# Softmax backward by row sums of P∘dP on VectorE instead of a product with O^T on TensorE, in a transformer block's backward pass

## The chip, the cores and the metric

The kernel runs on one core of one Trainium2 chip. The metric is device time in microseconds (us) of one execution, from launch to end. The engines are TensorE (PE, with its weight loads shown as PEld), VectorE (DVE), ScalarE (ACT), GpSimd (POOL) and SyncE (SP); SP and POOL also issue DMA transfers, in the order of their own queues, and a queue that waits for something holds everything behind it. One matmul reads its stationary operand (lhsT) as a weight load and streams the other (rhs) through the array.

## The reference, cut to what matters

One adaLN-modulated block, forward and all gradients: x + ga·A(h1), then x + gb·GLU(h2). A is attention over 64 segments of 32 tokens with a memory of 8 rows that the previous segment's output feeds, so segments follow each other, forward and, in reverse, backward.

```
for s in range(n_seg):                       # 64 segments, 32 heads of 128, L = 8 + 32 rows
    h = concat([mem, x[s]]);  q, k, v = h@Wq, h@Wk, h@Wv
    p = softmax(q k^T * scale + mask);  o = p v
    o = einsum(o, Wo);  mem = o[:8];  outs += o[8:]
# backward of one head's softmax, with dO given:
dV = P^T dO;  dP = dO V^T
dS = P * (dP - rowsum(P * dP)) * scale       # rowsum(P*dP) equals rowsum(O * dO)
dQ = dS K;  dK = dS^T Q;  dh = dQ Wq^T + dK Wk^T + dV Wv^T
```

The weight gradients (wgrad) of Wo, Wq, Wk, Wv are products over all 64·40 rows, made in a last phase.

## The kernel before, in words

The 32 heads are packed three to a group of 120 rows: 11 groups (`G`), each a 128x128 tile of a 128x1408 array. `PG = 4` groups share one PSUM bank, so work per segment goes in three parts (`NP = 3`) of 4, 4 and 3 groups.

**Phases.** Phase 2 is the forward pass, 64 segments in a row. For each it stores to DRAM the V^T columns (`VT`), the probabilities (`PS`), rows of Q and K (`QST`, `KST`), rows of O (`OSR`) and O^T (`OT`). Phase 3 is the GLU, forward and backward, a software pipeline of seven stages over 16 tiles of 128 rows, and its weight gradients. Phase 4 is attention backward, segments 63 down to 0. Phase 5 makes the weight gradients of the four attention matrices and the first layer norm's backward.

**Phase 4, one segment.** `col_pass` projects the incoming gradient dy by Wo^T to rows (`RAd`), `turn_half` transposes them, `to_heads` (ACT and DVE) writes the columns dO^T (`dOT`). POOL copies the rows into `dOst`. Then dP = dO V^T is started in PSUM (`dp`, L1405); DVE multiplies O^T by dO^T in place (`prod`, L1390); and 11 matmuls of that product against a tile of minus ones (`negones`, L1413) subtract rowsum(O∘dO) from dP in the same PSUM bank, so one DVE instruction per part (L1415) gives dS. PE goes on with dV (`grad_part("dVT")`, L1426), the transposes of dS (`dstt`, L1342, copied by DVE, L1440), dK, the product of dV^T with Wv^T (`dht`, L211, 32 column-tiled matmuls), dQ, and `dht` for dK and dQ. `fold_split` and `fold_sum` add the four column tiles and give the memory gradient, which the next segment's dy needs (`dyT`, L1525). dK leaves PSUM by DVE, dV and dQ by ACT.

Every fourth segment completes a batch of memory-row tails: `get_db` (POOL, L1182) copies its input `dyb`, `proj_b` projects it on PE in two halves, in the segments with s % 4 = 2 and 1, and `turn_b` transposes it where s % 4 = 0.

**Row stores.** Each of dV^T, dK^T, dQ^T is turned to rows by a DMA transpose on SP's queue into one of three buffers (`rows_x`), and POOL issues the store to DRAM (`DVR`, `DKR`, `DQR`, L1436). A segment ends with `store_rows_x(2)`, which issues its dV store; the next one issues the dK store after its `dOst` copies (`store_rows_x(1)`) and the dQ store later (`store_rows_x(0)`).

**Order.** In phases 2 and 4 `pin` fixes each engine's order as written. In phase 3 a planner orders the instructions by its own estimates of cost, within their dependencies. There, `s0` computes on POOL `db = dout * gb` (L904) and the reciprocal deviation `rstd` (L917), on which DVE's normalisation (L920) waits.

**Phase 5.** The gradients are made in chunks of at most four heads by 20 row pairs. The first Wo chunk has two heads (`rows_a`, loaded in segment 0 of phase 4 by `p5_first` into the memory of `WoT`), the second the other two of that group; their matmuls are L1744, those of the other three matrices L1731. `ln_tile` loads its own inputs (x0, dh, dx1) where it uses them, and its two small matmuls stand in PE's order between chunks (L1617, L1620).

Of the kernel before, what the change touches and what calls it, by code (L numbers as in the profile page):

```python
# [8 lines left out]
F32 = mybir.dt.float32  # L9
# [31 lines left out]
class K:  # L41
# [43 lines left out]
    def alloc_dram(self):  # L85
# [9 lines left out]
        self.OT = d("OT", GL, BF16)  # L95
# [308 lines left out]
    def phase2(self):  # L404
# [13 lines left out]
        with ExitStack() as ctx:  # L418
# [210 lines left out]
            for s in range(NS):  # L629
# [149 lines left out]
                nc.sync.dma_start(self.OT[s], gl3(OT))  # L779
# [52 lines left out]
    def phase3(self):  # L832
# [9 lines left out]
        with ExitStack() as ctx:  # L842
# [53 lines left out]
            def s0(j):  # L896
# [6 lines left out]
                db = sbp.tile([128, D], BF16, name="db", bufs=2)  # L903
                nc.gpsimd.tensor_tensor(db[:], st["dout"][:], gb_bc[:], op=ALU.mult)  # L904
                nc.gpsimd.dma_start(self.DBROWS[r0:r1, :], db[:])
# [10 lines left out]
                rstd = sbp.tile([128, 1], F32, name="rstd2", bufs=6)  # L916
                nc.gpsimd.tensor_tensor(rstd[:], ve[:], mhalf[:], op=ALU.pow)  # L917
                xh2 = sbp.tile([128, D], BF16, name="xh2", bufs=5)
# [236 lines left out]
    def p4_weights_setup_begin(self):  # L1155
        nc, tc, cfg, io = self.nc, self.tc, self.cfg, self.io
        D, DC, H, E = cfg.D, cfg.DC, cfg.H, cfg.E
        ctx = self.p4_ctx
        self.wo_ctx = ExitStack()
        wop = self.wo_ctx.enter_context(tc.tile_pool(name="p4wo", bufs=1, side="right", reuse_waits="tile"))  # L1160
        self.WoT = wop.tile([128, DC, H * E], BF16, name="WoT")
        wp = ctx.enter_context(tc.tile_pool(name="p4w", bufs=1, side="right", reuse_waits="tile"))
        self.negones = wp.tile([128, 128], BF16, name="negones")
        nc.gpsimd.memset(self.negones[:], -1.0)
        self.WqT = wp.tile([128, H, D], BF16, name="WqT")
        self.WkT = wp.tile([128, H, D], BF16, name="WkT")
        self.WvT = wp.tile([128, H, D], BF16, name="WvT")
        self.dyp = ctx.enter_context(tc.tile_pool(name="p4dy", bufs=3, side="right", reuse_waits="tile"))
        self.dap = ctx.enter_context(tc.tile_pool(name="p4da", bufs=2, side="right", reuse_waits="tile"))
        self.das, self.dbs = {}, {}  # L1170
# [62 lines left out]
    def phase4(self):  # L1233
# [7 lines left out]
        with self.p4_ctx as ctx:  # L1241
            WqT, WkT, WvT, WoT, negones = self.WqT, self.WkT, self.WvT, self.WoT, self.negones

            ldp = ctx.enter_context(tc.tile_pool(name="p4ld", bufs=2, reuse_waits="tile"))
# [28 lines left out]
            btd = pt.tile([128, 8, 128], BF16, name="btd")  # L1273
# [51 lines left out]
            def get_loads(s):  # L1325
                if s not in loads:
                    d = {}
                    for nm, dram in (("OT", self.OT), ("Pst", self.PS)):
                        t = ldp.tile([128, G * GW], BF16, name=nm + "_l")
                        nc.sync.dma_start(gl3(t), dram[s])  # L1330
                        d[nm] = t
# [42 lines left out]
            for s in reversed(range(NS)):  # L1374
# [9 lines left out]
                VT, OT, Pst, Kst, Qst = ld["VT"], ld["OT"], ld["Pst"], Kst_t, Qst_t  # L1384
# [3 lines left out]
                def prod(pi):  # L1388
                    n = min(PG, G - pi * PG)
                    nc.vector.tensor_tensor(part3(OT, pi)[:, :, 0:120],  # L1390
                                            dOT[:, pi * PG * 120:(pi * PG + n) * 120].rearrange("p (g x) -> p g x", x=120),
                                            part3(OT, pi)[:, :, 0:120], op=ALU.mult)
# [7 lines left out]
                def dp(pi):  # L1400
                    ps = dps[pi] = ps_f32("dp_ps")
                    n = min(PG, G - pi * PG)
                    for j in range(n):
                        g = pi * PG + j
                        nc.tensor.matmul(ps[:, j, :], lhsT=dOT[:, g * 120:g * 120 + GW], rhs=VT[:, g * 120:g * 120 + GW],  # L1405
                                         start=(j == 0), stop=False, skip_group_check=True)

                def ds(pi):
                    ps = dps[pi]
                    n = min(PG, G - pi * PG)  # L1410
                    for j in range(n):
                        g = pi * PG + j
                        nc.tensor.matmul(ps[:, j, :], lhsT=OT[:, g * GW:(g + 1) * GW], rhs=negones[:, :],  # L1413
                                         start=False, stop=True, skip_group_check=True)
                    nc.vector.scalar_tensor_tensor(out=part3(dS, pi), in0=ps[:, 0:n, :], scalar=cfg.scale, in1=part3(Pst, pi),  # L1415
                                                   op0=ALU.mult, op1=ALU.mult)
# [13 lines left out]
                def grad_out(nm, xt, pi, eng, ps):  # L1430
                    self.evac(eng, part3(xt, pi), ps[:, 0:min(PG, G - pi * PG), :])
# [30 lines left out]
                if s == 0:  # L1462
                    self.p5_first()
                late = None
# [12 lines left out]
                prod(0)  # L1477
                dp(0)
                prod(1)
                dp(1)  # L1480
                prod(2)
                ds(0)
                self.pop_later()
                dp(2)
                dost(2)
                ds(1)
                ds(2)
# [7 lines left out]
                grad_part("dVT", dOst, Pst, dVT, 0, "act")  # L1495
                grad_part("dVT", dOst, Pst, dVT, 1, "act")
                dstt(0)
                gk0 = grad_mm("dKT", Qst, dS, 0)
                grad_part("dVT", dOst, Pst, dVT, 2, "act")
                dstt(1)  # L1500
                gk1 = grad_mm("dKT", Qst, dS, 1)
                dstt(2)
                gk2 = grad_mm("dKT", Qst, dS, 2)
                load_rows(Qst_t, self.QST, s - 1)
                for pi, g in enumerate((gk0, gk1, gk2)):
                    grad_out("dKT", dKT, pi, "dve", g)
                for pi in range(NP):
                    dht(dVT, WvT, pi)
# [7 lines left out]
                if s > 0:  # L1516
                    store_rows_x(2)
# [25 lines left out]
    def p5_first(self):  # L1543
# [4 lines left out]
        self.rows_a = self.flat(self.WoT, NTP * D, NTP * 2 * E).rearrange("p (t x) -> p t x", t=NTP)  # L1548
# [3 lines left out]
        osr = lambda r, n, tl: self.OSR[:, r:r + n, 0:2, :].rearrange("s (tp tl) g e -> tl s tp (g e)", tl=2)[tl]  # L1552
        for a in (M // 2, M // 2 + tps):
            for tl in range(2):
                n = min(tps, T // 2 - a)
                nc.sync.dma_start(self.rows_a[tl * NS:(tl + 1) * NS, a:a + n, :], osr(2 * a, 2 * n, tl))
                if n < tps:
                    nc.sync.dma_start(self.rows_a[tl * NS:(tl + 1) * NS, a + n:NTP, :], osr(96, 8, tl))
                nc.sync.dma_start(self.dyrows[tl * NS:(tl + 1) * NS, a:a + tps, :],
                                  self.DAROWS[:, :].rearrange("(s tp tl) d -> tl s tp d", tp=T // 2, tl=2)[tl][:, a - M // 2:a - M // 2 + tps])  # L1560
        for tl in range(2):
            nc.sync.dma_start(self.rows_a[tl * NS:(tl + 1) * NS, 0:M // 2, :], osr(0, M, tl))
# [10 lines left out]
    def phase5(self):  # L1573
# [8 lines left out]
        with ExitStack() as ctx:  # L1582
            ctx.enter_context(self.wo_ctx)
            rp = ctx.enter_context(tc.tile_pool(name="p5g_r", bufs=1, side="right", reuse_waits="tile"))
# [16 lines left out]
            def ln_tile(j):  # L1601
                r0, r1 = j * 128, (j + 1) * 128
                x0 = sb2.tile([128, D], BF16, name="x0_5")
                nc.sync.dma_start(x0[:], x_rows[r0:r1, :])
                st = sb1.tile([128, 6], F32, name="st5")
# [9 lines left out]
                dhb = sb2.tile([128, D], BF16, name="dhb5")  # L1615
                self.load_x_rows(dhb, j, self.DHA, self.DHB)
# [4 lines left out]
                dx1 = sb2.tile([128, D], F32, name="dx1_5")  # L1621
                nc.sync.dma_start(dx1[:], self.DX1ROWS[r0:r1, :])
# [49 lines left out]
            if not getattr(cfg, "skip_wgrad", False):  # L1672
# [20 lines left out]
                o_chunks = [(0, 0, 2), (0, 2, 2)] + chunks[1:]  # L1693
# [21 lines left out]
                for i, (_, kind, outw, (hl, g0, ng)) in enumerate(todo):  # L1715
# [6 lines left out]
                    while ln_done[0] * (n_ln - 3) < (i - 3) * NT and ln_done[0] < NT:  # L1722
# [14 lines left out]
                    else:  # L1737
# [3 lines left out]
                        for part in parts:  # L1741
                            for gg in range(ng):
                                for tp_ in part:
                                    nc.tensor.matmul(pss[gg][:], lhsT=rows[:, tp_, gg * E:(gg + 1) * E], rhs=dyrows[:, tp_, :],  # L1744
# [183 lines left out]
```

## Time and profile before

| | |
|---|---|
| median of 7 runs | 3353.46 us (3346.57 to 3359.04) |
| the profiled execution | 3355.38 us; span of its trace 3353.6 us |
| phase 2 | about 39 to 1062 us |
| phase 3, pipeline and its weight gradients | about 1062 to 1645 us |
| phase 4 | about 1645 to 2737 us |
| phase 5 | about 2737 to the end |
| PE busy | 3030.6 us, 90% of the span |
| DVE, ACT, POOL busy | 1629.9, 1136.3, 1432.0 us |
| DMA | 699.38 MB moved, 209 GB/s over the span |
| O^T stores and loads | 64 of each, 352.0 KB each |

A group of the profile names its line, engine, operation, the tiles written and read, the count, the busy time and the mean of one; behind it the engine's idle time before it and what ended that. Overlapping instructions of one engine both count as long as they last, so the distance between two starts is what an instruction costs in a stream, and its duration is what a waiting engine sees.

### The profile page before, as it was taken

Reading aid. Unit: us, or ns where it says so; the run is one execution under the profiler, and the core shown is the slowest. Engines: PE = TensorE matmul, PEld = TensorE weight load, DVE = VectorE, ACT = ScalarE, POOL = GpSimd, SP = SyncE. Lnnn points to the kernel's source line nnn. Section 1 sums busy time; section 2 is a strip of 40 time slices with the busy share of each in tenths; the row PEclk is TensorE's granted clock in tenths of the full one; section 3 lists DMA queues with packets and bytes.
Section 4 is the critical chain, followed back from the end, with each engine's and each line's share of the span. In section 5 each row is a group of like instructions: output and inputs, shape, how many; then the busy total and the mean of one; then the engine's idle time right before and its main releaser. Section 6 shows DMA issues by size and latency. Waiting matters only on the chain. (4 is left out here: it accounts for less than half of the span.)

```text
span 3353.6 us, 95627 instructions
## 1 busy us (share of the span) xinstructions
PE 3030.6 (90%) x38574; PEld 1728.2 (52%) x38650; DVE 1629.9 (49%) x4298; ACT 1136.3 (34%) x2586; POOL 1432.0 (43%) x3037
## 2 busy tenths in 40 slices
PE   6999999999997899989989989998999978999999
PEld 3555555555554444445555555555555543444454
DVE  5556556666554777632345544455455531332211
ACT  3555555555543333322233333333333320110011
POOL 3556555655554555511344434344444431232321
PEclk8999999999998999999999999999999998999999
DMA  8655655555556798887699999999999999789886
GB/s 300 175 165 167 174 170 163 169 170 165 169 165 206 180 212 206 205 261 235 181 243 235 242 239 232 235 233 243 244 238 240 238 223 226 223 183 201 197 223 167
DMA packets 862015, 699.38 MB, mean 209 GB/s; under 512 B 560690, under 2 KB 734274, under 8 KB 861444
## 3 DMA queue, kind: packets, MB, share of 16 engines
q1 hardware_dynamic: 737220, 483.44, 61.3%
q0 software_dynamic: 52912, 147.43, 13.7%
q10 hardware_dynamic: 71440, 62.40, 7.2%
q8 instruction: 304, 4.98, 0.7%
q14 instruction: 139, 1.14, 0.1%
HBM read 293.60 MB, written 275.02 MB: 170 GB/s over the span
## 5 line engine op out<-in xcount | busy, mean ns | idle before, releaser
L1731 PE MATMUL gps<-rows,hrows 128*128 128x512 bf16 (+2 forms) x2124 | 416.9, 356 | 5.5 <-ACT ot L61 2.7
L1731 PEld LDWEIGHTS <-hrows 128*128 128x128 bf16 x2160 | 211.6, 98 | 209.5 <-issue 5.1
L222 PEld LDWEIGHTS <-hT 128*32 128x32 bf16 x6144 | 160.2, 98 | 187.1 <-ACT hT L785 30.5
L1436 POOL DMA_DIRECT2D DVR<-rows_x x64 | 35.7, 558 | 422.6 <-DMA rows_x<-dVT 422.6
L282 DVE TENSOR_TENSOR dh_lo<-dh_ps,dh_hi 128x256 bf16<-128x256 f32 x128 | 48.3, 419 | 317.5 <-ACT dh_hi L278 317.5
L1735 POOL DMA_DIRECT2D out_dram<-ot x108 | 81.2, 753 | 254.4 <-DVE ot L63 144.5
L63 DVE CAST ot<-gps 128x512 bf16<-128x512 f32 (+3 forms) x76 | 47.7, 632 | 261.9 <-PE gps L1731 106.1
L791 POOL TENSOR_TENSOR Pst<-Pst,rden 120x1408 bf16<-120x1408 bf16 x63 | 159.4, 2530 | 16.4 <-issue 8.3
L1744 PE MATMUL gps5o<-WoT,rows 128*128 128x512 bf16 x588 | 135.6, 390 | 22.5 <-DMA rows<-OSR 21.6
L222 PE MATMUL pass_ps<-Wv,hT 128*32 128x512 bf16 x2048 | 126.9, 391 | 24.0 <-ACT hT L785 24.0
L61 ACT ACTIVATE dQT<-g_ps 128x512 bf16<-128x512 f32 (+1 forms) x192 | 94.0, 562 | 157.7 <-issue 136.8
L61 ACT ACTIVATE ot<-gps 128x512 bf16<-128x512 f32 (+3 forms) x75 | 41.1, 548 | 312.2 <-PE gps L1731 131.7
L222 PE MATMUL pass_ps<-WoT,dyT 128*32 128x512 bf16 x2048 | 123.9, 384 | 22.5 <-ACT dyT L1525 22.5
L306 POOL DMA_DIRECT2D AOA<-at_rb x64 | 36.7, 574 | 249.5 <-DVE at_rb L305 135.9
L694 DVE TENSOR_TENSOR Ost<-or_ps,rden 120x512 bf16<-120x512 f32 (+1 forms) x192 | 124.2, 647 | 23.0 <-PE or_ps L692 2.2
L211 PE MATMUL dh_ps<-WvT,dVT 128*32 128x512 bf16 x2048 | 122.9, 382 | 0.0
L211 PE MATMUL dh_ps<-WkT,dKT 128*32 128x512 bf16 x2048 | 122.3, 381 | 0.0
L211 PE MATMUL at_ps<-Wo,OT 128*32 128x512 bf16 x2048 | 122.3, 381 | 0.0
L222 PE MATMUL pass_ps<-Wk,hT 128*32 128x512 bf16 x2048 | 122.2, 381 | 0.0
L211 PE MATMUL dh_ps<-WqT,dQT 128*32 128x512 bf16 x2048 | 121.6, 379 | 0.0
L222 PE MATMUL pass_ps<-Wq,hT 128*32 128x512 bf16 x2048 | 121.6, 379 | 0.0
L1460 POOL COPY dOst<-RAd 96x512 bf16<-96x512 bf16 x128 | 77.4, 616 | 96.5 <-DVE RAd L63 96.5
(409 smaller groups left out, 7295.1 us busy)
## 6 DMA issues: line engine op xcount, KB each, us to landing
OSR<-Ost SPq DMA_DIRECT2D x64, 352.0 KB
OT<-OT SPq DMA_DIRECT2D x64, 352.0 KB
PS<-Pst SPq DMA_DIRECT2D x64, 352.0 KB
OT_l<-OT SPq DMA_DIRECT2D x64, 352.0 KB
Pst_l<-PS SPq DMA_DIRECT2D x64, 352.0 KB
DVR<-rows_x POOLq DMA_DIRECT2D x64, 352.0 KB, 4.8
DKR<-rows_x POOLq DMA_DIRECT2D x64, 352.0 KB, 5.6
DQR<-rows_x POOLq DMA_DIRECT2D x64, 352.0 KB, 5.8
```

The source lines that it names most:

```text
L61: return nc.scalar.activation(out, in_, AF.Copy)
L63: return nc.vector.tensor_copy(out, in_)
L211: self.nc.tensor.matmul(ps[32 * j:32 * j + 32, :], lhsT=lhsT, rhs=w, start=(n < 4), stop=(n >= total - 4), tile_position=(0, 32 * j))
L222: self.nc.tensor.matmul(ps[32 * j:32 * j + 32, :], lhsT=lhs(c), rhs=rhs, start=(c == 0), stop=(c == DC - 1), tile_position=(0, 32 * j))
L282: nc.vector.tensor_tensor(lo[:], ps[:, 256 * h:256 * h + 256], parts[h][:], op=ALU.subtract)
L306: nc.gpsimd.dma_start(dram, rb[:])
L694: nc.vector.tensor_tensor(part3(Ost, pi)[0:120, 0:n, :], or_ps[0:120, 0:n, :], rden[:, pi * PG:pi * PG + n].unsqueeze(2).to_broadcast([120 ...
L791: nc.gpsimd.tensor_tensor(Pst[0:120, :, :], Pst[0:120, :, :], rden[:, :].unsqueeze(2).to_broadcast([120, G, 128]), op=ALU.mult)
L1460: nc.gpsimd.tensor_copy(dOst[0:96, 512 * hf:512 * hf + 512], RAd[0:96, 512 * hf:512 * hf + 512])
L1731: nc.tensor.matmul(ps[:, 0:ng * E], lhsT=hrows[:, tp_, c * 128:(c + 1) * 128], rhs=rows[:, tp_, 0:ng * E], start=(tp_ == 0), stop=(tp_ == ...
L1735: nc.gpsimd.dma_start(outw[c * 128:(c + 1) * 128, h0:h0 + 3 * (ng - 1) + 1:3, :], ot[:, 0:ng * E].rearrange("p (h e) -> p h e", e=E))
L1744: nc.tensor.matmul(pss[gg][:], lhsT=rows[:, tp_, gg * E:(gg + 1) * E], rhs=dyrows[:, tp_, :], start=(tp_ == order[0]), stop=(tp_ == order[ ...
```

## The change

Five parts.

1. O^T is no longer stored in phase 2 nor loaded in phase 4. `prod`, the matmuls with `negones` and the one DVE instruction per part are gone. DVE now makes, group by group, P∘dP with its row sum as an accumulated output (128x128 from PSUM), and then (dP − sum)∘P with that sum as a scalar per row: 22 instructions of 128x128 a segment. The factor `scale` moves to the evacuations of dK and dQ.
2. The order behind it: all three `dp` parts first, then all of `ds`; the dV matmuls; for each part the transposes of dS and dK, with the 32 `dht` matmuls of dV between the second and the third; dK leaves PSUM by ACT instead of DVE.
3. `store_rows_x(2)` at a segment's end is gone: the dV store is issued in the next segment, with the dK store, behind the `dOst` copies.
4. In phase 3 POOL's `db` and its store stand behind `rstd`, and the two instructions are tied in this order.
5. In phase 5 the first Wo chunk has four heads. Of its 20 row pairs 12 are loaded in segment 0 into `WoT`'s memory, two into `btd`, which now lives on into phase 5, and six already in segment 6 (`p5_early`). The layer norm's inputs are loaded one tile ahead (`ln_load`), and its tiles start a chunk later.

```
@@ phase 2
-                nc.sync.dma_start(self.OT[s], gl3(OT))
@@ phase 3, s0
-                db = sbp.tile([128, D], BF16, name="db", bufs=2)
-                nc.gpsimd.tensor_tensor(db[:], st["dout"][:], gb_bc[:], op=ALU.mult)
-                nc.gpsimd.dma_start(self.DBROWS[r0:r1, :], db[:])
...
+                i0 = len(self.traced())
                 nc.gpsimd.tensor_tensor(rstd[:], ve[:], mhalf[:], op=ALU.pow)
+                db = sbp.tile([128, D], BF16, name="db", bufs=2)
+                nc.gpsimd.tensor_tensor(db[:], st["dout"][:], gb_bc[:], op=ALU.mult)
+                self.pin(i0, [mybir.EngineType.Pool])
+                nc.gpsimd.dma_start(self.DBROWS[r0:r1, :], db[:])
@@ phase 4, loads and ds
-                    for nm, dram in (("OT", self.OT), ("Pst", self.PS)):
-                        t = ldp.tile([128, G * GW], BF16, name=nm + "_l")
-                        nc.sync.dma_start(gl3(t), dram[s])
-                        d[nm] = t
+                    d["Pst"] = ldp.tile([128, G * GW], BF16, name="Pst_l")
+                    nc.sync.dma_start(gl3(d["Pst"]), self.PS[s])
...
-                def prod(pi):
-                    n = min(PG, G - pi * PG)
-                    nc.vector.tensor_tensor(part3(OT, pi)[:, :, 0:120],
-                                            dOT[:, pi * PG * 120:(pi * PG + n) * 120].rearrange("p (g x) -> p g x", x=120),
-                                            part3(OT, pi)[:, :, 0:120], op=ALU.mult)
+                rsum = sb2.tile([128, G], F32, name="rsum")
...
                     for j in range(n):
                         g = pi * PG + j
-                        nc.tensor.matmul(ps[:, j, :], lhsT=OT[:, g * GW:(g + 1) * GW], rhs=negones[:, :],
-                                         start=False, stop=True, skip_group_check=True)
-                    nc.vector.scalar_tensor_tensor(out=part3(dS, pi), in0=ps[:, 0:n, :], scalar=cfg.scale, in1=part3(Pst, pi),
-                                                   op0=ALU.mult, op1=ALU.mult)
+                        junk = sb2.tile([128, GW], BF16, name="pdp")
+                        nc.vector.scalar_tensor_tensor(out=junk[:], in0=ps[:, j, :], scalar=1.0, in1=part3(Pst, pi)[:, j, :],
+                                                       op0=ALU.mult, op1=ALU.mult, accum_out=rsum[:, g:g + 1])
+                    for j in range(n):
+                        g = pi * PG + j
+                        nc.vector.scalar_tensor_tensor(out=part3(dS, pi)[:, j, :], in0=ps[:, j, :], scalar=rsum[:, g:g + 1],
+                                                       in1=part3(Pst, pi)[:, j, :], op0=ALU.subtract, op1=ALU.mult)
...
-                    self.evac(eng, part3(xt, pi), ps[:, 0:min(PG, G - pi * PG), :])
+                    nc.scalar.activation(part3(xt, pi), ps[:, 0:min(PG, G - pi * PG), :], AF.Copy,
+                                         scale=1.0 if nm == "dVT" else cfg.scale)
@@ phase 4, order of a segment
+                if s == 6:
+                    self.p5_early()
...
-                prod(0)
                 dp(0)
-                prod(1)
                 dp(1)
-                prod(2)
-                ds(0)
+                dp(2)
+                for pi in range(NP):
+                    ds(pi)
+                dost(2)
                 self.pop_later()
-                dp(2)
-                dost(2)
-                ds(1)
-                ds(2)
...
-                grad_part("dVT", dOst, Pst, dVT, 0, "act")
-                grad_part("dVT", dOst, Pst, dVT, 1, "act")
-                dstt(0)
-                gk0 = grad_mm("dKT", Qst, dS, 0)
-                grad_part("dVT", dOst, Pst, dVT, 2, "act")
-                dstt(1)
-                gk1 = grad_mm("dKT", Qst, dS, 1)
-                dstt(2)
-                gk2 = grad_mm("dKT", Qst, dS, 2)
+                for pi in range(NP):
+                    grad_part("dVT", dOst, Pst, dVT, pi, "act")
+                for pi in range(NP):
+                    dstt(pi)
+                    grad_part("dKT", Qst, dS, dKT, pi, "act")
+                    if pi == 1:
+                        for pj in range(NP):
+                            dht(dVT, WvT, pj)
                 load_rows(Qst_t, self.QST, s - 1)
-                for pi, g in enumerate((gk0, gk1, gk2)):
-                    grad_out("dKT", dKT, pi, "dve", g)
-                for pi in range(NP):
-                    dht(dVT, WvT, pi)
...
-                if s > 0:
-                    store_rows_x(2)
@@ phase 5
-        self.rows_a = self.flat(self.WoT, NTP * D, NTP * 2 * E).rearrange("p (t x) -> p t x", t=NTP)
+        n = NTP - 8
+        self.rows_a = self.flat(self.WoT, NTP * D, n * 4 * E).rearrange("p (t x) -> p t x", t=n)
...
+    def osr_rows(self, r, n, tl):
+        return self.OSR[:, r:r + n, 0:4, :].rearrange("s (tp tl) g e -> tl s tp (g e)", tl=2)[tl]
+
+    def p5_early(self):
+        NS, h = self.cfg.NS, self.cfg.T // 2
+        for tl in range(2):
+            self.nc.sync.dma_start(self.rows_x0[tl * NS:(tl + 1) * NS, 0:4, :], self.osr_rows(2 * (h - 4), 8, tl))
+            self.nc.sync.dma_start(self.rows_x0[tl * NS:(tl + 1) * NS, 4:6, :], self.osr_rows(96, 4, tl))
...
+            def ln_load(j):
+                if j >= NT or j in ln_in:
+                    return
...
             def ln_tile(j):
                 r0, r1 = j * 128, (j + 1) * 128
-                x0 = sb2.tile([128, D], BF16, name="x0_5")
-                nc.sync.dma_start(x0[:], x_rows[r0:r1, :])
+                ln_load(j)
+                ln_load(j + 1)
+                x0, dhb, dx1 = ln_in.pop(j)
...
-                o_chunks = [(0, 0, 2), (0, 2, 2)] + chunks[1:]
+                o_chunks = chunks
...
-                    while ln_done[0] * (n_ln - 3) < (i - 3) * NT and ln_done[0] < NT:
+                    if i == 3:
+                        ln_load(0)
+                    while ln_done[0] * (n_ln - 4) < (i - 4) * NT and ln_done[0] < NT:
                         ln_step()
```

## The prediction

> **What bounds the kernel now.** First the busy time by stage (columns: stretch, its length, then PE, PEld, DVE, ACT and POOL busy with instruction counts, granted TensorE clock, DMA share, GB/s). The rows are phase 2, phase 3's pipeline, phase 4, the turn into phase 5 and the rest.
>
> ```profile
> 39.00:1062.00 1023.00, 945.27 (x16574) 588.52 (x16571) 602.02 (x1896) 517.10 (x1302) 586.09 (x1412) 0.99 0.59 170
> 1062.00:1450.00 388.00, 339.74 (x1897) 167.97 (x1916) 260.08 (x449) 130.73 (x228) 199.94 (x216) 0.96 0.85 213
> 1645.00:2724.00 1079.00, 971.00 (x15680) 576.88 (x15681) 546.83 (x1482) 377.52 (x881) 448.06 (x1109) 0.98 1.06 237
> 2724.00:2923.00 199.00, 163.40 (x939) 74.74 (x949) 48.35 (x114) 18.45 (x33) 43.30 (x66) 0.91 0.93 217
> ```
>
> PE is the busy engine everywhere, so each stage is read by what PE waits for. DMA looks full in phase 4; the waits of PE there (total, times, longest) show that this hardly matters:
>
> ```profile
> PE dp_ps L1405 <- ACT dOT L61: 27.7, 63, 0.5
> PE pass_ps L222 <- POOL dyb L1182: 27.7, 13, 3.4
> PE pass_ps L222 <- ACT dyT L1525: 22.5, 63, 0.9
> PE dp_ps L1413 <- DVE OT_l L1390: 11.1, 56, 0.6
> PE g_ps L1426 <- POOL dOst L1460: 2.7, 4, 1.7
> PE dp_ps L1405 <- DMA VT_l<-VT: 2.5, 1, 2.5
> ```
>
> One wait for DMA in 1079 us. Two of the rows are POOL's lateness. The timeline of one segment shows the stretch that the change rewrites (start, length, engine, line), and below it POOL in another segment:
>
> ```profile
> 1957.74 0.46 PE L1405 MATMUL dp_ps<-VT_l,dOT 128*128 128x128 bf16 x5 [0.46 <-ACT dOT L61]
> 1957.92 0.97 DVE L1390 TENSOR_TENSOR OT_l<-dOT,OT_l 128x480 bf16<-128x480 bf16 x3
> 1958.81 1.75 DVE L1415 SCALAR_TENSOR_TENSOR dS<-dp_ps,Pst_l 128x512 bf16<-128x512 f32 x3
> 1961.59 1.91 PE L211 MATMUL dh_ps<-WvT,dVT 128*32 128x512 bf16 x32
> 1964.15 1.91 PE L211 MATMUL dh_ps<-WkT,dKT 128*32 128x512 bf16 x32
> ...
> 2005.05 0.56 POOL L1436 DMA_DIRECT2D DVR<-rows_x  x1 [9.59 <-DMA rows_x<-dVT]
> 2006.64 0.29 POOL L1182 COPY dyb<-daq 128x128 bf16<-128x128 bf16 x1
> 2006.98 1.05 PE L222 MATMUL pass_ps<-WoT,dyb 128*32 128x512 bf16 x16 [2.67 <-POOL dyb L1182]
> ```
>
> DVE needs 2.7 us for prod and dS, and PE fills them. From the resumed dp (1957.74) to dht of dK (1964.15) PE takes 6.41 us; two other segments show 6.47 and 6.26. The distance from one L1525 to the next gives segment lengths: at best 16.32, 16.43, 16.32 and 15.66 us for s % 4 = 0, 1, 2, 3, but the kind 2 averages 18.85 over 16. All surplus over the best of each kind is 50.5 us, 40.4 of it in kind 2, where POOL stood before the dV store.
>
> **Phase 4: the new row sums.** The price of one small DVE instruction comes from these rows:
>
> ```profile
> 1443.90 0.69 DVE L1015 SCALAR_TENSOR_TENSOR dxh<-mm,Wv 128x512 f32<-128x512 f32 x1 [0.58 <-ACT dh2b L1012]
> 1444.52 0.08 DVE L1015 DVE_READ_ACCUMULATOR dxh<-mm,Wv 128x1 f32 x1
> 1444.52 0.69 DVE L1018 TENSOR_TENSOR pr_cb<-mm,xh 128x512 bf16<-128x512 f32 x1
> 1445.12 0.68 DVE L1021 SCALAR_TENSOR_TENSOR junk<-dxh,xh 128x512 f32<-128x512 f32 x1
> 1445.97 0.74 DVE L1028 SCALAR_TENSOR_TENSOR ta<-dxh,rstd,Wv 128x512 f32<-128x512 f32 x1
> ```
>
> A plain pass of 512 from PSUM lasts 0.69 but the next starts after 0.60, 0.09 sooner; a 128x128 cast from PSUM (L299) lasts 0.289, so 0.20 in a stream. The accumulator adds 0.02 (0.62 against 0.60), a pointer scalar 0.05 (0.74 against 0.69). So the two kinds cost 0.22 and 0.25, mean 0.235; 22 make 5.17 us where prod and dS took 2.7. Bounds: 0.20 if both additions hide, 0.355 if nothing overlaps (0.289 plus 0.08, and 0.289 plus 0.05). I take 0.235, nearest to rows that read PSUM with an accumulator in a stream; each waits only for an instruction two or more back.
>
> Let T be the resumed dp. Its bank is readable at T+0.27 (0.23 of matmul, 0.04 to DVE). Sixteen instructions, two parts of dS, last 3.76, the last result 0.09 more: T+4.12. PE has by then done the rest of dp, dost, dV and the first dstt and dK, and idles some 1.6 us. Then the end of dstt(1) and dK(1) 0.34, dht of dV 1.84 (1961.59 to 1963.43 before), dstt(2) and dK(2) six at 0.057, dQ eleven at 0.057: dht of dK at T+7.27. The 11 negones matmuls (0.63) are already out of this. Against 6.26 to 6.47: +0.9 a segment, **+58 us** over 64; by the bounds +22 and +181. dS(2) and the copies of dS^T (0.34 apart) end about T+7.0, just ahead of the last dQ. In kind 1, DVE's evacuation of RBd stands ahead of the copies and adds 0.1.
>
> dK by ACT (0.6 and 0.55 an instruction): ACT has idle time there (dQT waited 136.8 us on "issue"), and only the last part precedes the dht that needs it; nothing. Its cover gone, 0.55 a segment. SP's dK transpose comes a little over 1 us later, and the Q load now stands behind it; that load has most of a segment until its use: nothing.
>
> **Phase 4: the late store.** What waits behind the dV store on POOL now (tail copies, dyb, dyT, dOst) goes ahead of it. In the segment shown the rows landed 3.35 us after the segment's start; POOL now comes to the store about 4.2 us after it, so the wait mostly ends. Behind it now are the dK store, the DHA store, the copies of the next dO^T tails, the dQ store and the three dOst transfers, needed some 10 us on. The next dV transpose may wait for its buffer by about 1 us, seen by SP alone. Gain between 27.7 (PE's own wait for dyb) and 50.5; I take 45, as dOst and what follows were late in the same segments: **-45 us**.
>
> O^T's stores and loads, 45 MB: PE's waits in phase 2 are compute waits but for 0.4 us, in phase 4 but for 2.5: 0, at most -3.
>
> **Phase 3.** In the pipeline's first tile PE lost 13.4 us:
>
> ```profile
> 1083.28 1.16 POOL L904 TENSOR_TENSOR db<-Wv 128x512 bf16<-128x512 bf16 x1 [7.97 <-DMA Wv<-in_grad_out_dram]
> 1094.31 0.58 POOL L917 TENSOR_TENSOR rstd<-ve,mhalf 128x1 f32<-128x1 f32 x1
> 1094.93 0.55 DVE L920 TENSOR_SCALAR xhf<-x,mv,rstd 128x512 f32<-128x512 f32 x1 [13.89 <-POOL rstd L917]
> ```
>
> Three db stood before the first rstd; now it can run at 1081. What is late next is h's transpose: SP has some 25 loads ahead of it at 0.35 each and now db's transpose too, so about 1094 instead of 1097.9: -4 (0 to -13.4). In the steady loop PE waits for du 22.6 us in 14 times, 0.74 at least: 12.2 to win. junk (L1021) takes 1.20 on average, 0.68 undisturbed: it meets POOL's umh, which now comes some 2 us sooner. -8, between -12 and +8, as db now meets h2a (a DVE pass beside db took 1.65 instead of 0.68). Together **-12**.
>
> **Phase 5.** PE waited 21.6 us for the second chunk's rows, and its next 11 matmuls took 4.85 us instead of 2.4 at the lower clock. Now 80 matmuls (17.3 us) come before a load is needed, but that load is twice as large: the chunk that started at 2786.0 gains only the 0.79 MB loaded early, 3.6 us at 217 GB/s: -4 (+3 to -10). The waits for dhb (8.4) and pr (2.4) go with loading ahead: -10 (0 to -10.8). Together **-14**.
>
> **Sum.** 58 - 45 - 12 - 14 = -13. The profiled execution's own time is 3355.4, so 3342; the median shown is 1.9 lower: 3340.
>
> A rule that speaks against it: the Trainium skill (VectorE: DVE Perf Modes, section "The TRN2 errata — SBUF-src ops pay a fixed extra latency per instruction") puts a PSUM-source pass at 120 cycles plus one per element at 0.96 GHz and advises tiles of 512 or more. As an estimate from that page, 128 elements are 0.258 us, which would add 24 us and end at 3364; the stream above shows 0.07 us of fixed cost, not 0.125.
>
> **Rivals.** (a) The small instructions overlap less: every nanosecond on 0.235 costs 16 x 64 = 1 us, so 13 ns more already takes the gain away, and 0.29 gives 3340 + 56 = 3396, slower. For it: 14 of the 22 wait on their own engine. Against it: those they wait for are long through. (b) POOL's wait moves: the dK store, DHA and the dO tails queue behind the dV store, and only 25 come back: 3360. Against: the next use is far off. (c) The additions hide, 0.20: 3340 - 36 = 3304. That the change only saves traffic is in the forecast as 0.
>
> **How the numbers follow.** Forecast 0.48, its own range 3318 to 3362; (a) 0.20, (b) 0.12, (c) 0.20. The range 3298 to 3392 reaches (c) and most of (a). A measurement tells about 0.2%, 6.7 us. Faster: 0.37 of the forecast and all of (c), 0.58. Same: 0.10 and 0.04 of (b), with 0.01 of (a), 0.15. Slower: 0.27.
>
> **What would show it.** dp resumed to dht of dK near 7.3 us; DVE's pairs near 0.22 and 0.25; kind 2 about 17.3 us and no long waits before DVR; xhf's first wait gone; PE's wait for dhb gone, and a wait of some 17 to 20 us for the second chunk. A segment stretch over 7.5 us, or POOL still waiting 400 us, makes it wrong.

## The result, and the profile after

The changed kernel takes 3367.2 us (median of 18 runs, 3357.7 to 3377.4) against 3352.7 for the kernel before (44 runs beside it): ratio 1.0041, 95% interval 1.0031 to 1.0052. It is 14 us slower; 3340 had been forecast. The profiled run is one of the shorter ones, 3361.4 us (span 3359.4).

The stages of the changed kernel, in the same windows as before (stretch, length, then PE, PEld, DVE, ACT and POOL busy, granted clock, DMA share, GB/s):

```profile
39.00:1062.00 1023.00, 945.28 (x16574) 588.33 (x16567) 599.97 (x1892) 515.55 (x1299) 584.62 (x1411) 0.99 0.53 148
1062.00:1450.00 388.00, 346.51 (x1970) 171.57 (x1987) 270.72 (x459) 133.50 (x234) 204.98 (x224) 0.97 0.88 222
1645.00:2724.00 1079.00, 957.93 (x14615) 522.49 (x14614) 586.30 (x2895) 456.82 (x1041) 435.08 (x1070) 0.99 0.92 211
2724.00:2923.00 199.00, 173.44 (x1177) 80.73 (x1187) 54.18 (x178) 27.72 (x55) 47.11 (x79) 0.96 0.97 219
```

DMA moves less in phases 2 and 4 (148 against 170 GB/s, 211 against 237), and neither shows a gain: PE does the same work in phase 2's window as before (945.28 against 945.27 us). In phase 4's window PE does 1065 fewer matmuls; 704 of these (11 times 64) can be the ones with `negones`, the others have moved behind its end, so phase 4 has become longer. The turn into phase 5 does more. By the first and the last of the 63 ACT copies of dyT in phase 4, 62 segments apart, the span divides so:

| | before | after | difference | predicted |
|---|---|---|---|---|
| up to the first dyT | 1664.8 | 1654.0 | -10.8 | -12 |
| 62 segments of phase 4 | 1054.2 | 1087.6 | +33.4 | +58 - 45 = +13 |
| from the last dyT to the end | 634.6 | 617.8 | -16.8 | -14 |

The 19 us between the sum (3342) and this profiled run (3361.4) lie in phase 4. PE's waits there, after the change:

```profile
PE tps L1341 <- DVE dS L1414: 29.0, 61, 0.7
PE dp_ps L1400 <- ACT dOT L61: 28.3, 62, 0.5
PE pass_ps L221 <- ACT dyT L1516: 21.9, 62, 0.6
PE g_ps L1425 <- ACT dOst L61: 14.4, 46, 0.7
PE tps L1341 <- ACT dVT L1430: 2.4, 15, 0.2
```

The wait for dyb (27.7 us before) is gone, and one for dS of much the same size stands in its place. These rows show only the matmuls; the weight loads of the same transposes waited 89.8 us for dS, in 336 gaps. From the resumed dp to dht of dK, an undisturbed segment of the changed kernel takes 7.45 us (1834.67 to 1842.12); 7.27 had been forecast, and the kernel before took 6.41 in the segment that the prediction shows:

```profile
1834.67 0.69 PE L1400 MATMUL dp_ps<-VT_l,dOT 128*128 128x128 bf16 x8 [0.47 <-ACT dOT L61]
...
1839.22 1.91 PE L210 MATMUL dh_ps<-WvT,dVT 128*32 128x512 bf16 x32
...
1842.12 1.91 PE L210 MATMUL dh_ps<-WkT,dKT 128*32 128x512 bf16 x32
```

The segment ahead of it is a disturbed one (start, length, engine, line):

```profile
1816.25 0.29 DVE L1410 SCALAR_TENSOR_TENSOR pdp<-dp_ps,Pst_l 128x128 bf16<-128x128 f32 x1
1816.46 0.08 DVE L1410 DVE_READ_ACCUMULATOR pdp<-dp_ps,Pst_l 128x1 f32 x1
1816.46 0.28 DVE L1410 SCALAR_TENSOR_TENSOR pdp<-dp_ps,Pst_l 128x128 bf16<-128x128 f32 x1
...
1817.10 1.12 DVE L1414 SCALAR_TENSOR_TENSOR dS<-dp_ps,rsum,Pst_l 128x128 bf16<-128x128 f32 x4
...
1818.13 0.28 DVE L1410 SCALAR_TENSOR_TENSOR pdp<-dp_ps,Pst_l 128x128 bf16<-128x128 f32 x1
...
1819.37 1.00 PE L1341 MATMUL tps<-ident,dS 128*128 128x128 bf16 x4 [0.54 <-DVE dS L1414]
1820.53 3.58 PE L210 MATMUL dh_ps<-WvT,dVT 128*32 128x512 bf16 x32
```

VectorE does what was predicted: one row-sum instruction starts 0.21 us after the other (forecast 0.22), the four dS take 1.03 from the first to the next instruction's start, 0.26 each (forecast 0.25). But the 32 matmuls of dht of dV take 3.58 us here; in the segment behind it, shown above, they take 1.91. The windows around them show why (same columns as above):

```profile
1813.74:1817.15 3.41, 2.94 (x47) 1.93 (x45) 2.03 (x15) 1.52 (x4) 3.02 (x7) 1.00 1.09 291
1817.15:1820.56 3.41, 2.45 (x26) 1.29 (x27) 3.41 (x23) 2.23 (x5) 2.85 (x8) 1.00 1.00 389
1820.56:1823.97 3.41, 3.41 (x33) 1.06 (x32) 2.20 (x8) 0.60 (x1) 0.00 (x0) 0.50 0.86 122
1823.97:1827.38 3.41, 3.41 (x65) 2.14 (x65) 0.36 (x1) 1.85 (x4) 1.02 (x3) 1.00 0.33 62
```

For 3.41 us the granted clock is 0.50, and 1.70 us of PE's work is lost. The 3.41 us before it are the stretch in which PE waits for dS: PE is recorded busy for 2.45 us of them and VectorE throughout. In the profiled run this strikes 9 of the 62 segments, 106 to 140 us apart; those take 18.6 to 19.2 us, the others a steady 17.32, 17.49, 17.49 and 16.95 us for s % 4 = 0, 1, 2, 3.

The Trainium skill (TensorE: Matmul & The Clock Gate, "What's actually happening") tells of a free-running window of 3413 ns after which the clock is halved or restored; the 3.41 us at 0.50 agree. Its section "Why this matters for your kernels" warns of gaps of PE above some 3 us. Here the longest gap in the window was 0.54 us, so for this kernel the trace decides: many short gaps were enough, as the same page's "A second HAM failure mode: psum-queue depth-cycling" says of another kernel.

### The profile page after: what moved, and what is told of

It is laid out like the page before. It is cut to its first block, busy times and chain, and to the rows that moved or that the text cites. A ratio compares the mean times of both kernels' runs of the same rounds, so it can differ in the third digit from the quotient of the medians.

```text
span 3359.4 us, 95805 instructions
## 1 busy us (share of the span) xinstructions
PE 3041.2 (91%) x37870; PEld 1686.9 (50%) x37946; DVE 1696.1 (50%) x5834; ACT 1229.6 (37%) x2778; POOL 1435.7 (43%) x3036
## 4 chain that ended last, share of the span: by engine, by line
PE 36%; DMA 7%; DVE 7%; issue 4%; ACT 2%; POOL 1%; SPq 1%; ACTq 0%; POOLq 0%; DVEq 0%
PE dh_ps L210 10%; PE gps L1745 6%; PE pass_ps L221 4%; DVE pdp L1410 3%; PE gps L1143 3%; DVE dS L1414 2%; DMA rows<-OSR 2%; PE tps L1341 2%; PE dh_tps L210 2%; PE g_ps L1425 2%; PE gps5o L1764 2%; PE turn_ps L230 1%; DMA rows<-DKR 1%; ACT dOT L61 1%; PE dh_ft L290 1%
## 5 line engine op out<-in xcount | busy, mean ns | idle before, releaser
L1414 DVE SCALAR_TENSOR_TENSOR dS<-dp_ps,rsum,Pst_l 128x128 bf16<-128x128 f32 x704 | 198.6, 342 | 0.0
L1430 ACT ACTIVATE dKT<-g_ps 128x512 bf16<-128x512 f32 (+1 forms) x192 | 108.5, 565 | 196.4 <-PE g_ps L1425 192.1
L789 POOL TENSOR_TENSOR Pst<-Pst,rden 120x1408 bf16<-120x1408 bf16 x63 | 159.4, 2531 | 16.8 <-issue 8.6
L1410 DVE SCALAR_TENSOR_TENSOR pdp<-dp_ps,Pst_l 128x128 bf16<-128x128 f32 x704 | 162.3, 284 | 0.3 <-PE dp_ps L1400 0.2
L1341 PE MATMUL tps<-ident,dS 128*128 128x128 bf16 x704 | 112.4, 226 | 44.8 <-DVE dS L1414 29.7
L210 PE MATMUL dh_ps<-WvT,dVT 128*32 128x512 bf16 x2048 | 137.4, 416 | 0.0
L1764 PE MATMUL gps5o<-WoT,rows 128*128 128x512 bf16 x549 | 125.5, 389 | 11.7 <-DMA rows<-OSR 11.2
```

Source lines behind the costliest of these rows:

```text
L210: self.nc.tensor.matmul(ps[32 * j:32 * j + 32, :], lhsT=lhsT, rhs=w, start=(n < 4), stop=(n >= total - 4), tile_position=(0, 32 * j))
L789: nc.gpsimd.tensor_tensor(Pst[0:120, :, :], Pst[0:120, :, :], rden[:, :].unsqueeze(2).to_broadcast([120, G, 128]), op=ALU.mult)
L1341: nc.tensor.transpose(ps[:, j, :], src[:, g * w:g * w + GW], self.ident[:, :])
L1410: nc.vector.scalar_tensor_tensor(out=junk[:], in0=ps[:, j, :], scalar=1.0, in1=part3(Pst, pi)[:, j, :], op0=ALU.mult, op1=ALU.mult, accum_ ...
L1414: nc.vector.scalar_tensor_tensor(out=part3(dS, pi)[:, j, :], in0=ps[:, j, :], scalar=rsum[:, g:g + 1], in1=part3(Pst, pi)[:, j, :], op0=AL ...
L1430: nc.scalar.activation(part3(xt, pi), ps[:, 0:min(PG, G - pi * PG), :], AF.Copy, scale=1.0 if nm == "dVT" else cfg.scale)
```

## The experiments

The theory after the first trace: the late store, phase 3 and phase 5 gained what was forecast, and the row sums cost about 80 us instead of 58: some 65 by VectorE's chain and some 15 by halved clock. Rivals: the gains overlap or moved elsewhere; the halved clock is chance. All runs, with the length from the first to the last dyT of the profiled run and the windows of halved clock in it:

| kernel | median us | ratio to before, 95% | 62 segments, us | halved |
|---|---|---|---|---|
| before | 3352.7 | | 1054.2 | 13 |
| changed | 3367.2 | 1.0041 (1.0031 to 1.0052) | 1087.6 | 9 |
| late_only | 3311.1 | 0.9864 (0.9848 to 0.9881) | 1008.0 | 1 |
| rows_only | 3393.6 | 1.0105 (1.0087 to 1.0122) | 1091.4 | 11 |
| old_p5 | 3376.9 | 1.0061 (1.0047 to 1.0075) | 1086.2 | 8 |
| keep_ot | 3287.0 | 0.9793 (0.9777 to 0.9810) | 1006.3 | 1 |
| p3_only | 3341.3 | 0.9968 (0.9951 to 0.9984) | 1047.6 | 12 |
| dht_early | 3331.5 | 0.9931 (0.9910 to 0.9952) | 1050.2 | 0 |
| wide_ds | 3314.1 | 0.9874 (0.9846 to 0.9901) | 1031.1 | 1 |
| early_store | 3367.7 | 1.0047 (1.0030 to 1.0063) | 1087.6 | 9 |
| pe_fill | 3632.0 | 1.0829 (1.0806 to 1.0851) | 1353.2 | 87 |
| pe_fill2 | 3352.1 | 0.9997 (0.9985 to 1.0008) | 1074.2 | 1 |
| rows_best | 3316.3 | 0.9893 (0.9874 to 0.9911) | 1036.8 | 0 |

**The late store alone** (late_only), the kernel before with

```diff
-                if s > 0:
-                    store_rows_x(2)
```

> The kernel before, with only the late dV store: store_rows_x(2) at the end of a segment is left out. Theory (POOL standing at the dV store is what makes segments of kind s % 4 = 2 long): the surplus over the best segments, 50.5 us, falls by 40 to 47, the long waits of POOL before DVR go, and the whole loses 40 to 47 us, 3306 to 3313 against 3353, ratio 0.986 to 0.988. Rival (the wait moves to another of POOL's transfers or copies): only 25 us, ratio 0.9925. Rival (half of the surplus is halved TensorE clock, 24 us of it, that would come at other places): 26 us, ratio 0.992.

Measured: 45.6 us faster (3311.1 against 3356.7 beside it). POOL's waits in phase 4, first in the kernel before, then with the late store alone:

```profile
POOL DVR L1436 <- DMA rows_x<-dVT: 415.3, 63, 10.6
POOL dOst L1460 <- DVE RAd L63: 96.5, 62, 5.3
```

```profile
POOL dOst L1460 <- DVE RAd L63: 387.1, 126, 6.6
POOL dh_tail L1802 <- ACT dQT L61: 72.0, 61, 1.5
```

POOL now waits for this segment's own RAd instead of the last segment's rows, and segments of kind 2 (s % 4 = 2) fall from 18.85 to 16.41 us on average. The rival that halved clock would come back elsewhere falls: 13 halved windows become 1. So some 20 of the 45 us that POOL's wait cost (12 times 1.70) were halved clock behind it, and went with the wait.

**The row sums alone** (rows_only): the kernel before with the row sums, the new order and ScalarE's evacuation of dK, nothing else of the change.

```diff
-                        nc.tensor.matmul(ps[:, j, :], lhsT=OT[:, g * GW:(g + 1) * GW], rhs=negones[:, :],
-                                         start=False, stop=True, skip_group_check=True)
+                        nc.vector.scalar_tensor_tensor(out=junk[:], in0=ps[:, j, :], scalar=1.0, in1=part3(Pst, pi)[:, j, :],
+                                                       op0=ALU.mult, op1=ALU.mult, accum_out=rsum[:, g:g + 1])
...
```

> The kernel before, with the row sums on VectorE and the new order of dV, dK and dht, but with the dV store, phase 3 and phase 5 as before. Theory (each segment is 1.0 to 1.2 us longer, 70 us over 63, and the idle between dp and dht of dV halves the TensorE clock in some 8 to 10 windows at 1.70 us each): +84 to +88, ratio 1.025. Rival (the longer segment leaves time for the dV rows to land, so POOL's wait shrinks although the store is where it was, and the late store gains little next to the row sums): +40 to +55, ratio 1.012 to 1.016. By the predicted terms alone it would be +58.

Measured: +35 us by the ratio (1.0105), +37 by the medians (3393.6 against 3356.7 beside it), a little below the rival's range and far from the theory's 84. The segments have the lengths of the changed kernel, 17.0 to 17.5 us, with 11 halved windows; kind 2 is as short as the others although the store is where it was. The next run asks the same from the other side.

**The store put back in the changed kernel** (early_store):

```diff
+                if s > 0:
+                    store_rows_x(2)
                 for pi in range(NP):
                     dht(dQT, WqT, pi)
```

> The changed kernel with the dV store back at the end of its own segment (before dht of dQ), all else as changed. Theory (with segments of 17.0 to 17.5 us the rows of dV have mostly landed when POOL comes to the store, so that the gain of the late store, 45 us in the kernel before, is mostly gone beside the row sums): 3 to 8 us slower than the changed kernel, ratio to before 1.005 to 1.0065. Rival (the terms add, as the prediction's sum has it): 45 us slower, 3412, ratio 1.0175.

Measured: 3367.7, no different from the changed kernel. POOL still waits for the rows (first line, phase 4), but the copy of dyb behind the store comes without a wait and in good time:

```profile
POOL DVR L1436 <- DMA rows_x<-dVT: 91.5, 20, 5.8
```

```profile
2003.02 0.56 POOL L1436 DMA_DIRECT2D DVR<-rows_x  x1
...
2004.62 0.29 POOL L1180 COPY dyb<-daq 128x128 bf16<-128x128 bf16 x1
2004.85 0.26 POOL L1295 COPY dyT<-daq 128x96 bf16<-128x96 bf16 x1
```

So the late store's 45 us and the row sums' cost are not two independent effects: with the row sums in place, POOL's wait for the rows no longer holds up the next segment. What brings this about is only in part seen. In the kinds 2, 0 and 3 the store follows the dyT that starts the segment by 17.6 to 18.7 us on average in the kernel before and by 13.0 to 13.7 here; POOL comes to it later (13.0 to 13.2 us instead of 9.9 to 12.2), so the rows themselves land sooner. No run separates the longer segment, the new order and the O^T loads that are gone. The forecast's sum was right to start from the best segments of the kernel before and to add the row sums to those, but the changed kernel owes nothing to the late store.

**O^T kept, with the rest of the change** (keep_ot): the late store, db behind rstd, the LN loads ahead. The four-head first chunk is not in it.

> The kernel before with its O^T way of the row sums, plus the late dV store, the db behind rstd in phase 3, and the loads ahead for the LN tiles in phase 5 (the first chunk stays as before, as the four-head buffers do not fit beside O^T). Theory (the row sums on VectorE cost about 86 us and all else of the change gains about 72): 45 + 11 + 10 = 66 us faster than before, 3287, ratio 0.980. Rival (the gains are partly the same idle time, moved by the later work): 40 us faster, ratio 0.988.

Measured: 3287.0, ratio 0.9793. It is the fastest kernel here, 2.4% below the changed one, and its distance of 80 us from the changed kernel is what the row sums cost, with the new order and ScalarE's evacuation of dK (less the four-head chunk, which it lacks). The 62 segments, where the chunk plays no part, differ by 81.3 us. Its segments are those of late_only.

**Phase 3 alone** (p3_only), the kernel before with db moved behind rstd.

> The kernel before with only db moved behind rstd in phase 3. Theory (rstd of the first tile no longer waits for three db, and junk meets POOL's umh less often): 8 to 12 us faster, ratio 0.9967, as the two profiled runs differ by 10.8 us up to phase 4. Rival (those 10.8 us are the former O^T stores or halved-clock windows that fall otherwise): 0 to 4 us, ratio 0.999 to 1.000.

Measured: 11 us faster by the ratio, 0.9968 (0.9951 to 0.9984), 12 by the medians, as the theory and the prediction had it. PE's waits in phase 3, before and then with this one part:

```profile
PE mm L952 <- DVE du L973: 22.6, 14, 3.6
PE tp L869 <- DVE Wq L63: 14.3, 3, 13.4
```

```profile
PE mm L954 <- DVE du L975: 17.1, 14, 3.6
PE mm L950 <- DMA hdT<-h: 8.6, 1, 8.6
PE tp L869 <- DVE Wq L63: 3.8, 2, 2.4
```

The 13.4 us become 8.6 us of waiting for h's transpose, which had been named as next late, and junk on DVE falls from 1203 to 784 ns on average, which was the reason given for the steady loop's share.

**Phase 5 as before in the changed kernel** (old_p5).

> The changed kernel with the former first chunk and the former loads of the LN tiles in phase 5. Theory (the 16.8 us that phase 5 lost between the two profiled runs come from the four-head chunk and the loads ahead): 17 us slower than the changed kernel, about 3384 against its 3367, ratio to before 1.009. Rival (8.5 of the 16.8 us are fewer windows of halved clock that happen to fall otherwise): 8 us slower, ratio 1.0065.

Measured: 9.7 us slower than the changed kernel by the medians, 6.7 by the ratios (1.0061 against 1.0041). So by these times phase 5's part is worth 7 to 10 us, not 16.8. The profiles say more: from the last dyT to the end the seven profiled kernels with the new phase 5 take 616.3 to 624.9 us, the five with the former 632.1 to 635.1, 13 us apart on average. Less halved clock about the turn into phase 5 is in this difference (granted clock 0.91 in the window 2724 to 2923 before, 0.96 after). The rival had it fall otherwise by chance; but the profiles with the new phase 5 have 5.5 to 10.0 windows' worth of it behind the last dyT, those with the former 9.1 to 11.6, so some of it goes with the change.

**Filling PE's idle time** (pe_fill): needless transposes ahead of the first and second part of dstt.

```diff
+                for j in range(fill):
+                    nc.tensor.transpose(ps[:, 0, :], dOT[:, j * 120:j * 120 + GW], self.ident[:, :])
...
-                    ps = transposes_part(dS, pi)
+                    ps = transposes_part(dS, pi, GW, (3, 8, 0)[pi])
```

> The changed kernel with 11 needless transposes of dO^T a segment (3 ahead of the first part of dstt, 8 ahead of the second), overwritten by the ones that follow: they only fill about 0.6 us of PE's idle time. Theory (a window of 3.4 us in which PE is idle for a third or more is followed by one of the same length at clock 0.50, 1.70 us lost): the 8 to 10 halved windows in the segments go, undisturbed segments stay at 17.3 to 17.5 us, 12 to 16 us faster than the changed kernel, about 3353, ratio 1.000. Rival (the halved windows do not hang on this idle time): no gain, or up to 7 us lost where the fillers are in the way, ratio 1.004 to 1.006.

Measured: 265 us slower than the changed kernel. The fillers read dO^T, and POOL's copies of the next segment's tails into dO^T stand ahead of them in the program, so PE had to wait for POOL:

```profile
1962.27 0.50 PE L1340 MATMUL tps<-ident,dOT 128*128 128x128 bf16 x3 [4.25 <-POOL dOT L65]
```

It answers nothing on the question, but 43 of the 62 segments have a stretch of 13.6 to 14.2 us, and there are two halved windows for each of these: long idle time and halved clock go together here.

**The same fillers from the P tile** (pe_fill2), which nobody writes meanwhile:

```diff
-                    nc.tensor.transpose(ps[:, 0, :], dOT[:, j * 120:j * 120 + GW], self.ident[:, :])
+                    nc.tensor.transpose(ps[:, 0, :], fill_src[:, j * GW:(j + 1) * GW], self.ident[:, :])
```

> The changed kernel with the same 11 needless transposes a segment as before, but of the P tile, which lies in SBUF since the segment before and is not written meanwhile (the earlier ones read dO^T, which POOL overwrites for the next segment, so that PE waited 4.25 us for POOL). Theory (idle time of PE in the stretch is what halves the clock in the window after it): no segment with a halved window, segments of 17.0 to 17.5 us throughout, 12 to 16 us faster than the changed kernel, about 3352, ratio 1.000. Rival (the halved windows come from something else, or the fillers are in the way): 3367 or above, ratio 1.004 or more.

Measured: 3352.1, ratio 0.9997 (0.9985 to 1.0008): 704 needless matmuls make the kernel 15 us faster. The undisturbed segments keep their lengths, 17.33, 17.49, 17.49 and 16.95 us, and of the 9 halved windows one is left. Over the same 1000 us of phase 4, the changed kernel and then this one:

```profile
1700.00:2700.00 1000.00, 889.57 (x13620) 486.33 (x13616) 549.07 (x2710) 424.54 (x969) 405.84 (x999) 0.99 0.93 212
```

```profile
1700.00:2700.00 1000.00, 915.84 (x14410) 524.66 (x14413) 554.12 (x2736) 433.40 (x981) 409.46 (x1008) 1.00 0.93 214
```

So what PE has to do in this stretch decides whether the clock is halved behind it: with a little more work there, at unchanged lengths of the segments, 8 of 9 windows are gone. At 1.70 us each they are 13.6 us of the 15. How much idle time it takes stays open (see the last section).

**dS in wide instructions** (wide_ds): three second passes instead of eleven, without the subtraction.

```diff
-                        nc.vector.scalar_tensor_tensor(out=part3(dS, pi)[:, j, :], in0=ps[:, j, :], scalar=rsum[:, g:g + 1],
-                                                       in1=part3(Pst, pi)[:, j, :], op0=ALU.subtract, op1=ALU.mult)
+                    nc.vector.scalar_tensor_tensor(out=part3(dS, pi), in0=ps[:, 0:n, :], scalar=1.0, in1=part3(Pst, pi),
+                                                   op0=ALU.mult, op1=ALU.mult)
```

> The changed kernel with dS made by one instruction of 512 for each part instead of four of 128 (three instead of eleven); the row sums are still formed but not subtracted, so the gradients through the softmax leave that term out. Theory (the small instructions on VectorE set the stretch): 8 of the 16 on the path, 2.08 us, become 2 of 0.60 us, the stretch falls by 0.88 us to 6.55, 56 us over 64 segments, and with the idle the halved windows go, 14 us more: 3297, ratio 0.983. Rival (the evacuations by ScalarE or the new order of PE's work bound the stretch): less than 30 us gained, ratio above 0.995.

Measured: 53 us faster than the changed kernel (3314.1). The stretch is 6.75 us in nearly every segment instead of 7.45, and there is one halved window. The rival falls: VectorE's small instructions do set the stretch. Why it is 0.70 us instead of 0.88 isn't shown: the four transposes of a part now all come behind one instruction, where three could go ahead before (three at 0.057 us are 0.17, an estimate), and PE's waits name ScalarE's evacuation of dK for 11.4 us.

**dht of dV one step earlier** (dht_early):

```diff
-                    if pi == 1:
+                    if pi == 0:
                         for pj in range(NP):
                             dht(dVT, WvT, pj)
```

> The changed kernel with dht of dV moved one step forward, ahead of the second part of dstt and dK instead of behind it. Theory (PE idles in the stretch because its work that does not need the row sums comes too late, not because VectorE is full): PE does dht of dV from 2.85 us after the resumed dp to 4.7 us, while VectorE makes the second and third part of dS; the stretch to dht of dK falls from 7.45 to 6.6 us where no RBd copy stands on VectorE and 7.1 us where it does, 44 us in all, and the windows of halved clock go, 14 us more: 3309, ratio 0.987. Rival (VectorE's chain up to the last copy of dS^T sets the end, so PE only waits later, at dQ): 0 to 15 us gained, ratio 1.000 to 1.004.

Measured: 36 us faster than the changed kernel, and 0.7% faster than the kernel before; between theory and rival. No window is halved in the segments; the stretch falls to 6.9 to 7.4 us, less than the theory had: the third part of dK now waits for a PSUM tile from ScalarE (15.1 us in 45 times), and dQ runs beside VectorE's last copies of dS^T. How much each takes isn't shown.

**The same, with two copies of dS^T on ScalarE** (rows_best):

```diff
-                    nc.vector.tensor_copy(part3(dST, pi), ps)
+                    self.evac("dve" if pi == NP - 1 else "act", part3(dST, pi), ps)
```

> The changed kernel with dht of dV one step forward, as in the run before, and the first two copies of dS^T on ScalarE instead of VectorE. Theory (what is left of the stretch, 6.9 to 7.4 us, is VectorE's tail: the third part of dS, RBd and three copies): the stretch falls to 6.3 to 6.7 us, 0.4 us a segment, 3306, ratio 0.986, still behind the 3287 of the kernel that keeps O^T. Rival (ScalarE, which now stands between PE and the PSUM buffers of dK, is as late): no change against 3331, ratio 0.993.

Measured: 3316.3, another 15 us; the stretch is 6.7 to 7.0 us where 6.3 to 6.7 was expected. This way of forming the row sums can be made to beat the kernel before by 1.1%, but not the kernel that keeps O^T, which lies 0.9% lower still.

## Why the prediction was wrong

- **What bounds the kernel** and where the change acts: right. No stage shows a gain from the missing O^T traffic: up to the first dyT, rows_only, which has no O^T stores either, takes 1668.9 us against 1664.8. Whether the missing loads help the dV rows to land sooner in phase 4 stays open.
- **"+0.9 a segment, +58 us over 64"**: this is the step that failed. The price of the instructions was right to the hundredth (0.21 and 0.26, mean 0.235; sixteen and the two parts of dS in 3.77 us against 3.76). The stretch measured 7.45 instead of 7.27: dht of dV began 0.09 later, and the 17 matmuls behind it took 1.06 instead of 0.97 us. By segments this makes 1087.6 - 9 x 1.65 - 1008.0 = 64.7 us, where 0.9 x 62 is 56 (1.65 is what a segment with a halved window is longer, 19.14 against 17.49). The larger miss is a term that was not in the sum: the 9 halved windows, 15 us, put at nothing without a reason. The prediction itself had PE "idle some 1.6 us" in the stretch, and counted that idle time only at its own length. Together the row sums cost 80 us instead of 58. Alone, wide_ds takes back 53 of these and dht_early 36; what the new order costs without the row sums was not measured.
- **The late store, -45**: -45.6 when made alone. Beside the row sums it is worth nothing (early_store). The sum did not suffer by it, as it counted the row sums from segments that were free of POOL's wait; a reader who takes the terms as separate gains would be misled.
- **Phase 3, -12**: right, in total and in its steps (the next wait is h's transpose; junk gets shorter).
- **Phase 5, -14**: 7 to 10 by the times, 13 by the profiles; near in total, but by other steps. The second chunk's wait fell from 21.6 to 11.2 us, more than the 4 taken. The waits for dhb and pr did not go, as these lines of the kernel before and then of the changed kernel show:

```profile
PE gps5o L1744 <- DMA rows<-OSR: 21.6, 1, 21.6
PE acc_ps L1617 <- DMA dhb<-DHB: 8.4, 2, 6.9
PE acc_ps L1620 <- POOL pr L1619: 2.4, 3, 1.2
```

```profile
PE gps5o L1764 <- DMA rows<-OSR: 11.2, 1, 11.2
PE acc_ps L1631 <- DMA dhb<-DHB: 5.2, 2, 4.2
PE acc_ps L1634 <- POOL pr L1633: 2.3, 2, 1.4
```

- **The rivals**: (a) was wrong, the small instructions overlap as assumed, and (c) with it; of (b) nothing was seen, POOL does not wait for the rows at all in the changed kernel. The result lies on the side of (a) for a reason that none of them held. The estimate from the Trainium skill's rule (VectorE: DVE Perf Modes, "The TRN2 errata — SBUF-src ops pay a fixed extra latency per instruction") came to 3364, close to the result, but by luck: its 0.258 us an instruction is not what the trace shows (0.21 and 0.26 from start to start).
- The sum that would have been right: 80 - 45 - 12 - 9 = +14, as measured; its terms are known to a few us each. The profiled run of the changed kernel, at 3361, is 6 us below its median; across its runs the granted clock goes from 0.979 (3377 us) to 0.983 (3357 us), which fits a number of halved windows that differs from run to run (it was counted in the profiled runs alone).

## What to carry to other kernels

When a change puts many short waits on PE into one stretch, add the chance of halved clock behind it to the price: in this kernel 1.70 us for each window, which made 15 us of the 80. Work on PE that does not depend on the slow engine belongs into that stretch; moving one such block one step forward was worth 36 us here. A gain that is real alone can be worth nothing beside another change (the late store, 45 us and 0), so each part is best measured alone and then beside the others.

## What the runs showed that was not expected

Halved clock comes in pieces of 3.41 us that cost 1.70 us each, in regular segments too in which the longest gap of PE in the window ahead was 0.54 us (0.60 in one). The changes of the clock lie whole multiples of 3.41 us apart throughout, so the windows in between are known. Of the four windows of the changed kernel that follow, the first is followed by halved clock; the third has more idle time on record and is not:

```profile
1940.02:1943.43 3.41, 2.47 (x27) 1.54 (x30) 3.41 (x21) 2.51 (x6) 0.00 (x0) 1.00 0.95 375
1943.43:1946.85 3.42, 3.42 (x32) 1.04 (x32) 1.68 (x8) 0.60 (x1) 2.11 (x7) 0.50 0.68 115
1974.15:1977.56 3.41, 2.26 (x28) 1.69 (x29) 2.93 (x20) 2.06 (x5) 2.16 (x4) 1.00 1.02 362
1977.56:1980.98 3.42, 3.01 (x44) 1.69 (x47) 3.42 (x21) 1.86 (x4) 0.00 (x0) 1.00 0.61 147
```

So the recorded busy time, whose ends are modelled, does not draw the limit, nor does the "third or more" of idle time that was supposed for pe_fill. The number of matmuls comes nearer: the nine windows ahead of halved clock have 19 to 27 on record, those with up to 73% of recorded busy time that were followed by full clock 27 to 31. Where the limit lies stays open. Eleven needless transposes a segment took the changed kernel from 3367 to 3352 us.
